# Exchanging the stationary and the streamed operand of P·V, with two V buffers in place of three, in a cached-attention kernel

## Chip, cores, metric

One core of one Trainium2 chip. The metric is the device time of one execution in microseconds (us), as the median over several executions. The profile's span is about 1.8 us shorter than the time of the same run.

## The reference, cut to what matters

```python
# x (8, 4, 448); k_cache, v_cache (8, 8, 8192, 256); wq (448, 4096); wo (4096, 448); all bf16
q = (x @ wq).reshape(8, 4, 16, 256).transpose(0, 2, 1, 3)
k = jnp.repeat(k_cache, 2, axis=1)          # 16 query heads share 8 kv heads
v = jnp.repeat(v_cache, 2, axis=1)
p = softmax(einsum("bhqd,bhkd->bhqk", q, k) * 256 ** -0.5)
o = einsum("bhqk,bhkd->bhqd", p, v)
return o.transpose(0, 2, 1, 3).reshape(8, 4, 4096) @ wo
```

There are 64 items, one per (batch, kv head). Each reads 4 MB of K and 4 MB of V and has only 8 query rows (2 heads x 4 positions).

## The kernel before

All loads are issued by SyncE on one queue, in chunks of 1 MB, K and V alternating. K goes through a ring of six chunk buffers, V through three buffers of a whole item.

```python
for n in range(NIT + 1):                    # NIT = 64 items, NCH = 4 chunks each
    ...                                     # alternating: kdma(n, c), vdma(n - 1, c)
def kdma(n, c):
    e.wait_ge(s_kfree[ks], ku)              # six ring slots
    ...
def vdma(m, pc):
    vs = m % NVBUF                          # NVBUF = 3
    if pc == 0 and m >= NVBUF:
        e.wait_ge(s_pv, m - NVBUF + 1)      # P.V of item m - NVBUF is done
    ...
```

TensorE transposes K tile by tile through PSUM (`stage`; VectorE and ScalarE copy the result to `KT_sb`), multiplies with Q (`ST`), and one item later does the softmax statistics, P·V and the denominator. P·V keeps a V tile stationary and streams P, which it repeats 8 times:

```python
def pe_pv(e, m):
    ...                                     # waits: exp of m, norm of m - 1, V of m
    for half in range(2):
        for t in range(NT):                 # NT = 64 tiles of 128 keys
            pe_mm(e, OT_ps[:, half * OTW:(half + 1) * OTW],
                  lhsT=V_sb[vs][:, t, half * P:(half + 1) * P],
                  rhs=PT_sb[m % 2][:, None, t * QN:(t + 1) * QN].to_broadcast([P, PVREP, QN]),
                  start=(t == 0), stop=(t == NT - 1), ...)     # PVREP = 8, QN = 8

def pe_den(e, m):                           # column sums of P, on all partitions
    pe_mm(e, ST_ps[m % 2][:, 0:NT * QN], lhsT=ones[:, :], rhs=PT_sb[m % 2][:, :], ...)

def dve_part2(e, m):                        # sum over tiles, reciprocal, scale into attnT
    ...

# the end of the TensorE program, after the last K tile
pe_maxT(NIT - 1); pe_bc(NIT - 1)            # P.V of item NIT - 2 came just before
pe_pv(e, NIT - 1); pe_den(e, NIT - 1)
...                                         # 32 matmuls with wo
```

## Time and profile before

Median 1341.24 us of 3 runs (1340.98 to 1341.73).

| what | before |
|---|---|
| bytes in the data queue | 544.3 MB |
| that queue's share of 16 DMA engines | 97.4% |
| TensorE busy, mean clock | 82%, 0.90 |
| packets and bytes of TensorE's instruction queue | 196, 3.21 MB |
| last V chunk landed | 1323.31 us |
| from there to the end of the span | 16.9 us |

The page of the kernel before. The rows of part 2 have one entry for each of 40 equal slices of the span: `DMA` is the busy share of the 16 engines in tenths, `GB/s` what they moved, `PEclk` TensorE's clock in tenths. Part 3 lists the queues: packets, MB, share of 16 engines. In all views PE is TensorE, PEld its weight loads, DVE VectorE, ACT ScalarE, POOL GpSimd and SPq the load queue of SyncE; L139 is line 139 of the kernel file.

```profile
PE 1093.5 (82%) x24932; PEld 1050.4 (78%) x24932; DVE 542.3 (40%) x1161; ACT 556.8 (42%) x577; POOL 0.8 (0%) x7
...
PEclk9969899888998998899898898898898999798998
DMA  7999999999999999999999999999999999999992
GB/s 263 424 411 425 424 424 423 424 425 424 423 425 424 424 424 425 423 423 424 425 423 424 414 419 424 413 422 421 410 424 422 419 419 417 421 410 423 422 399 96
...
q1 hardware_dynamic: 78464, 544.30, 97.4%
q8 instruction: 196, 3.21, 0.9%
```

Between the first slice and the last two, the DMA engines are busy for 90% of the time or more in every slice: this is a DMA-bound kernel. What the average hides is the end. Here is the windows view of the last stretch of loading (start:end, length, then busy time of each engine, clock, DMA share, GB/s):

```profile
1304.00:1321.00 17.00, 10.96 (x293) 10.20 (x290) 5.98 (x15) 5.63 (x6) 0.00 (x0) 0.94 0.51 213
```

For 17 us only half of the DMA capacity is in use. The landing events of the trace say which half: every chunk raises its semaphore sixteen times, and 50 us before the landing of the last chunk eight of these come within about 1 us and the other eight 17 to 19 us later. At 72 us into the run the sixteen lie within 1.7 us; the gap between the eighth and the ninth then grows to 15.4 us at about 1000 us and little after that (16.6 us at 1290 us). So eight of sixteen engines fall behind, and the kernel ends when they end. I call them the late half.

The chain of waits of the kernel before, from the last V load on (start us, length us, what):

```profile
1295.89 27.42 DMA V_sb<-in_v_cache_dram
...
1323.45 6.48 PE bankO L139 x128
1329.93 0.23 PE ST L139
...
1330.18 0.70 DVE dsum L244
...
1330.91 0.21 DVE rden L247
...
1331.14 0.25 DVE attnT L253 x2
...
1331.44 6.24 PE stage L139 x32
...
1337.70 0.61 DVE out_sb L470
```

After the last V chunk come P·V (6.48 us), the denominator matmul with its reduction and reciprocal (1.14 us), the scaling, and the output projection. An ordinary P·V (at 1274 us) took 3.88 us in the chain of waits; this one ran at a low clock.

Three of the costliest groups (line, engine, operation, output<-inputs, shape, count | busy us, mean ns | idle us before them and what ended it):

```profile
L139 PE MATMUL stage<-ident,kq_sb 128*128 128x128 bf16 x5440 | 462.6, 233 | 121.1 <-DMA kq_sb<-in_k_cache_dram 109.3
...
L139 PE MATMUL stage<-ident,K_sb 128*128 128x128 bf16 x2752 | 246.4, 242 | 70.2 <-DMA K_sb<-in_k_cache_dram 65.3
L139 PE MATMUL bankO<-PT_sb,V_sb 128*128 128x64 bf16 x8192 | 266.5, 197 | 14.2 <-issue 10.5
```

TensorE waited 109.3 + 65.3 = 175 us for K, 2.7 us per item of about 20.4 us. It is the second-busiest engine and not the bound. The waits of the load queue itself (who waits <- for whom: us in all, times, longest us):

```profile
SPq L299 <- PE ST L139: 468.0, 213, 5.2
```

This is the K load waiting for a free ring slot. V loads (line 308) do not appear in this view: three V buffers are plenty.

### The profile page before, as it was taken

How to read it: one execution, taken by the hardware profiler on the slowest of the kernel's cores; microseconds unless marked ns; L12 is line 12 of the kernel's file. 1: busy time of each engine (PE TensorE's matmuls, PEld its weight loads, DVE VectorE, ACT ScalarE, POOL GpSimd, SP SyncE). 2: the span in 40 equal slices, each digit the busy share in tenths (PEclk: the TensorE clock that was granted, in tenths of full speed). 3: DMA queues.
4: the chain of work that ended last, by engine and by line, in shares of the span. 5: the costliest groups of instructions: out<-in, count | busy, mean ns of one | idle time of the engine just before them, and what ended most of it. 6: DMA issues, size and time to landing. Idle time of an engine off the chain costs nothing.

```text
span 1340.2 us, 53869 instructions
## 1 busy us (share of the span) xinstructions
PE 1093.5 (82%) x24932; PEld 1050.4 (78%) x24932; DVE 542.3 (40%) x1161; ACT 556.8 (42%) x577; POOL 0.8 (0%) x7
## 2 busy tenths in 40 slices
PE   5878788788788878888878888888888788887886
PEld 4868778788778878877878788878888778787785
DVE  1424344343443443444344443443443444343442
ACT  1524444443443443443444444443443444443441
POOL 0000000000000000000000000000000000000000
PEclk9969899888998998899898898898898999798998
DMA  7999999999999999999999999999999999999992
GB/s 263 424 411 425 424 424 423 424 425 424 423 425 424 424 424 425 423 423 424 425 423 424 414 419 424 413 422 421 410 424 422 419 419 417 421 410 423 422 399 96
DMA packets 78688, 547.74 MB, mean 409 GB/s; under 512 B 8320, under 2 KB 12480, under 8 KB 12480
## 3 DMA queue, kind: packets, MB, share of 16 engines
q1 hardware_dynamic: 78464, 544.30, 97.4%
q8 instruction: 196, 3.21, 0.9%
q14 instruction: 28, 0.23, 0.0%
HBM read 544.24 MB, written 0.03 MB: 406 GB/s over the span
## 4 chain that ended last, share of the span: by engine, by line
DMA 63%; PE 28%; SPq 5%; DVE 2%; issue 2%
DMA kq_sb<-in_k_cache_dram 34%; DMA K_sb<-in_k_cache_dram 25%; PE stage L139 14%; PE bankO L139 8%; PE ST L139 4%; DMA V_sb<-in_v_cache_dram 2%; SPq L284 2%; SPq L308 2%; SPq L299 1%; DVE rmax L422 1%; DMA kq_sb<-in_wq_dram 1%; PE ST L344 1%; PE misc L139 1%; DVE KT_sb L231 1%; DVE dsum L244 0%
## 5 line engine op out<-in xcount | busy, mean ns | idle before, releaser
L229 ACT ACTIVATE KT_sb<-stage 128x1024 bf16<-128x1024 bf16 x512 | 523.7, 1023 | 756.8 <-PE stage L139 756.0
L139 PE MATMUL stage<-ident,kq_sb 128*128 128x128 bf16 x5440 | 462.6, 233 | 121.1 <-DMA kq_sb<-in_k_cache_dram 109.3
L231 DVE COPY KT_sb<-stage 128x1024 bf16<-128x1024 bf16 x512 | 351.1, 690 | 441.3 <-PE stage L139 440.6
L139 PEld LDWEIGHTS stage<-ident,kq_sb 128*128 128x128 bf16 x5440 | 347.1, 104 | 137.1 <-DMA kq_sb<-in_k_cache_dram 116.3
L139 PE MATMUL ST<-QT_sb,KT_sb 128*128 128x8 bf16 x8192 | 368.2, 168 | 16.5 <-issue 16.1
L139 PEld LDWEIGHTS ST<-QT_sb,KT_sb 128*128 128x128 bf16 x8192 | 336.7, 100 | 19.7 <-issue 19.5
L139 PE MATMUL stage<-ident,K_sb 128*128 128x128 bf16 x2752 | 246.4, 242 | 70.2 <-DMA K_sb<-in_k_cache_dram 65.3
L139 PE MATMUL bankO<-PT_sb,V_sb 128*128 128x64 bf16 x8192 | 266.5, 197 | 14.2 <-issue 10.5
L139 PEld LDWEIGHTS bankO<-PT_sb,V_sb 128*128 128x128 bf16 x8192 | 259.0, 101 | 15.7 <-issue 13.3
L139 PEld LDWEIGHTS stage<-ident,K_sb 128*128 128x128 bf16 x2752 | 185.6, 108 | 79.8 <-DMA K_sb<-in_k_cache_dram 69.6
L244 DVE TENSOR_REDUCE dsum<-ST 128x8 f32<-128x512 f32 x64 | 44.3, 692 | 308.8 <-PE ST L139 308.8
L444 DVE TENSOR_TENSOR D_sb<-ST,bc_sb 128x512 f32<-128x512 f32 x64 | 44.3, 692 | 2.2
L422 DVE TENSOR_REDUCE rmax<-ST 128x8 f32<-128x512 f32 x64 | 43.6, 681 | 1.0 <-PE ST L139 1.0
L478 ACT ACTIVATE PT_sb<-D_sb 128x512 bf16<-128x512 f32 x64 | 39.8, 622 | 8.5 <-DVE D_sb L444 8.5
L139 PE MATMUL ST<-PT_sb,ones 128*128 128x512 bf16 x64 | 24.4, 381 | 0.7 <-issue 0.7
L344 PE MATMUL ST<-xT_sb,kq_sb 128*128 128x32 bf16 (+1 forms) x128 | 10.7, 197 | 11.1 <-DMA kq_sb<-in_wq_dram 11.1
L344 PEld LDWEIGHTS ST<-xT_sb,kq_sb 128*128 128x128 bf16 (+1 forms) x128 | 8.3, 107 | 13.5 <-issue 11.2
L139 PE MATMUL misc<-ident,rmax_bf 128*8 128x128 bf16 x64 | 14.1, 221 | 5.8 <-DVE rmax_bf L427 1.5
L431 DVE TENSOR_REDUCE gmax<-misc 8x1 f32<-8x128 bf16 x64 | 17.2, 269 | 2.4 <-PE misc L139 2.4
L253 DVE TENSOR_TENSOR attnT<-bankO,rden 128x8 bf16<-128x8 f32 x128 | 15.4, 161 | 2.3
L434 DVE TENSOR_SCALAR diag<-ident,gmax 8x8 bf16<-8x8 bf16 x64 | 13.9, 217 | 2.3
L247 DVE RECIPROCAL rden<-dsum 128x8 f32<-128x8 f32 x64 | 13.0, 203 | 2.2
(21 smaller groups left out, 64.3 us busy)
## 6 DMA issues: line engine op xcount, KB each, us to landing
V_sb<-in_v_cache_dram SPq DMA_DIRECT2D x256, 1024.0 KB, 22.8
kq_sb<-in_k_cache_dram SPq DMA_DIRECT2D x170, 1024.0 KB, 25.9
K_sb<-in_k_cache_dram SPq DMA_DIRECT2D x86, 1024.0 KB, 25.9
wo_sb<-in_wo_dram SPq DMA_DIRECT2D x2, 1792.0 KB, 31.0
kq_sb<-in_wq_dram SPq DMA_DIRECT2D x3, 1024.0 KB, 6.8
kq_sb<-in_wq_dram SPq DMA_DIRECT2D x1, 512.0 KB, 11.4
x_sb<-in_x_dram SPq DMA_DIRECT2D x1, 28.0 KB, 1.7
out_dram<-out_sb SPq DMA_DIRECT2D x1, 28.0 KB, 1.5
```

The lines of the kernel that those rows point to most:

```text
L139: ins = e.matmul(*args, **kwargs)
L229: ins = e.activation(out=dst, in_=src, func=ACTF.Copy)
L231: ins = e.tensor_copy(out=dst, in_=src)
L244: chain(e, e.tensor_reduce(out=dsum[:, :], in_=ST_ps[m % 2][:, 0:NT * QN].rearrange("p (j q) -> p q j", q=QN), axis=AX.X, op=ALU.add))
L253: ins = e.tensor_tensor(out=attnT[:, c0:c0 + 2, b * Sq:(b + 1) * Sq], in0=OT_ps.rearrange("p (half rq) -> p half rq", half=2)[:, :, r * Sq ...
L284: e.dma_start(wo_sb[:, half_c:, :], wo_v[:, half_c:, :]).then_inc(s_wo, 16)
L308: e.dma_start(V_sb[vs][:, pc * TV:(pc + 1) * TV, :], src).then_inc(s_v[vs], 16)
L344: ins = e.matmul(bank[:, col:col + NR], lhsT=wq_sb[0:w, kc, hc * P:(hc + 1) * P], rhs=xT_sb[0:w, kc, :], start=(kc == 0), stop=(kc == NDC ...
L422: chain(e, e.tensor_reduce(out=rmax[:, :], in_=st[:, 0:NT * QN].rearrange("p (j q) -> p q j", q=QN), axis=AX.X, op=ALU.max))
L431: chain(e, e.tensor_reduce(out=gmax[0:QN, :], in_=MAXT_ps, axis=AX.X, op=ALU.max))
L444: e.tensor_tensor(out=D_sb[m % 2][:, :].rearrange("p (j q) -> p j q", q=QN), in0=st[:, 0:NT * QN].rearrange("p (j q) -> p j q", q=QN), in1 ...
L478: e.activation(out=PT_sb[m % 2][:, :], in_=D_sb[m % 2][:, :], func=ACTF.Exp, scale=scale).then_inc(s_exp, 1)
```

## The change

P becomes stationary (8 columns) and V is streamed (256 columns), so that P·V is 64 matmuls instead of 128. The output then has 8 rows of 256; it is normalized there, and two small transposes bring it to the layout that the output projection wants. The denominator gets its own small VectorE path. One V buffer is given up; the scratch space does not need it, since d_nv3 below ran with three. The last two items keep the old form, but with the denominators moved ahead and fifteen dummy matmuls (`fill`) between the softmax steps.

```diff
-    NVBUF = 3
-    PVREP = 8
+    NVBUF = 2
...
         def pe_pv(e, m):
...
-            for half in range(2):
-                for t in range(NT):
-                    pe_mm(e, OT_ps[:, half * OTW:(half + 1) * OTW],
-                          lhsT=V_sb[vs][:, t, half * P:(half + 1) * P],
-                          rhs=PT_sb[...].to_broadcast([P, PVREP, QN]), ...)
+            for t in range(NT):
+                pe_mm(e, O_ps,                                   # 8 x 256
+                      lhsT=PT_sb[m % 2][:, t * QN:(t + 1) * QN],
+                      rhs=V_sb[vs][:, t, :], ...)
...
+        def pe_ot(e, m):                                         # 2 transposes of 8x128
+        def dve_den(e, m):     # mask with ident, reduce, reciprocal: 8x512
+        def dve_on(e, m):      # O_n = O_ps * rden8, 8x256
+        def dve_otcopy(e, m):  # into attnT
...
-            pe_maxT(NIT - 1)
-            pe_bc(NIT - 1)
-            pe_pv(e, NIT - 1)
-            pe_den(e, NIT - 1)
+            pe_den_vs(e, NIT - 2)
+            fill(9)
+            pe_maxT(NIT - 1)
+            fill(6)
+            pe_bc(NIT - 1)
+            pe_pv_vs(e, NIT - 2)
+            pe_den_vs(e, NIT - 1)
+            pe_pv_vs(e, NIT - 1)
```

More of the change, by code (lines that the diff above doesn't have):

```diff
@@ L90, in bass_standalone__gqa_block_cached__sampling_kernel @@
         rden = sb("rden", [P, QN], FP32)
+        den8 = sb("den8", [P, 1], FP32)
+        rden8 = sb("rden8", [P, 1], FP32)
+        scr = sb("scr", [P, NT * QN], FP32)
+        O_n = [sb(f"O_n{i}", [P, Dh], BF16) for i in range(2)]
         out_sb = sb("out_sb", [P, D], BF16)
@@ L97, in bass_standalone__gqa_block_cached__sampling_kernel @@
         misc_f = misc[:, :].bitcast(FP32)
-        OTW = PVREP * QN
-        OT_ps = bankO[:, 0:2 * OTW]
+        O_ps = bankO[0:QN, 0:Dh]
+        OT2_ps = misc[:, 192:192 + 2 * QN]
         FIN_ps = stage[0][:, :].bitcast(FP32)[0:NR, 0:D]
@@ L127, in bass_standalone__gqa_block_cached__sampling_kernel @@
         s_norm = sem("s_norm")
+        s_on = sem("s_on")
+        s_ot = sem("s_ot")
         s_dve = sem("s_dve")
@@ L199, in pe_den @@
             e.wait_ge(s_exp, m + 1)
-            pe_mm(e, ST_ps[m % 2][:, 0:NT * QN], lhsT=ones[:, :], rhs=PT_sb[m % 2][:, :],
+            pe_mm(e, ST_ps[m % 2][0:QN, 0:NT * QN], lhsT=ones[:, 0:QN], rhs=PT_sb[m % 2][:, :],
                   start=True, stop=True, inc=s_den)
@@ L206, in pe_pv, with pe_den_vs, pe_pv_vs @@
             if m >= 1:
+                e.wait_ge(s_on, m)
+            e.wait_ge(s_v[vs], 16 * NCH * (m // NVBUF + 1))
+            for t in range(NT):
+                pe_mm(e, O_ps,
+                      lhsT=PT_sb[m % 2][:, t * QN:(t + 1) * QN],
+                      rhs=V_sb[vs][:, t, :],
+                      start=(t == 0), stop=(t == NT - 1),
+                      inc=(s_pv if t == NT - 1 else None))
+        OTW = 8 * QN
+        OT_ps = bankO[:, 0:2 * OTW]
+        def pe_den_vs(e, m):
+            e.wait_ge(s_exp, m + 1)
+            pe_mm(e, ST_ps[m % 2][:, 0:NT * QN], lhsT=ones[:, :], rhs=PT_sb[m % 2][:, :],
+                  start=True, stop=True, inc=s_den)
+        def pe_pv_vs(e, m):
+            vs = m % NVBUF
+            e.wait_ge(s_exp, m + 1)
+            if m == NIT - 2:
+                e.wait_ge(s_on, m)
+            else:
                 e.wait_ge(s_norm, m)
@@ L211, in pe_pv @@
                     last_one = (half == 1 and t == NT - 1)
-                    pe_mm(e,
-                          OT_ps[:, half * OTW:(half + 1) * OTW],
+                    pe_mm(e, OT_ps[:, half * OTW:(half + 1) * OTW],
                           lhsT=V_sb[vs][:, t, half * P:(half + 1) * P],
-                          rhs=PT_sb[m % 2][:, None, t * QN:(t + 1) * QN].to_broadcast([P, PVREP, QN]),
-                          start=(t == 0), stop=(t == NT - 1),
-                          inc=(s_pv if last_one else None))
+                          rhs=PT_sb[m % 2][:, None, t * QN:(t + 1) * QN].to_broadcast([P, 8, QN]),
+                          start=(t == 0), stop=(t == NT - 1), inc=(s_pv if last_one else None))
+        def pe_ot(e, m):
+            e.wait_ge(s_on, m + 1)
+            if m >= 1:
+                e.wait_ge(s_norm, m)
+            for h in range(2):
+                pe_mm(e, OT2_ps[:, h * QN:(h + 1) * QN],
+                      lhsT=O_n[m % 2][0:QN, h * P:(h + 1) * P], rhs=ident[0:QN, 0:QN],
+                      is_transpose=True, start=True, stop=True,
+                      inc=(s_ot if h == 1 else None))
         def evac(e, n, g, use_act):
@@ L239, in chain, with dve_part2_vs @@
             e.wait_ge(s_dve, dv_count[0])
-        def dve_part2(e, m):
+        def dve_den(e, m):
+            e.wait_ge(s_den, m + 1)
+            chain(e, e.tensor_tensor(
+                out=scr[0:QN, :].rearrange("p (j q) -> p j q", q=QN),
+                in0=ST_ps[m % 2][0:QN, 0:NT * QN].rearrange("p (j q) -> p j q", q=QN),
+                in1=ident[0:QN, None, 0:QN].to_broadcast([QN, NT, QN]),
+                op=ALU.mult))
+            chain(e, e.tensor_reduce(
+                out=den8[0:QN, 0:1], in_=scr[0:QN, :].rearrange("p (j q) -> p j q", q=QN),
+                axis=AX.XY, op=ALU.add))
+            chain(e, e.reciprocal(rden8[0:QN, :], den8[0:QN, :]))
+        def dve_on(e, m):
+            e.wait_ge(s_pv, m + 1)
+            if m >= 2:
+                e.wait_ge(s_ot, m - 1)
+            e.tensor_scalar(out=O_n[m % 2][0:QN, :], in0=O_ps, scalar1=rden8[0:QN, 0:1],
+                            scalar2=None, op0=ALU.mult).then_inc(s_on, 1)
+        def dve_part2_vs(e, m):
             b, hkv = m // Hkv, m % Hkv
@@ L250, in dve_part2 @@
             for r in range(rep):
-                h = hkv * rep + r
-                c0 = h * 2
+                c0 = (hkv * rep + r) * 2
                 ins = e.tensor_tensor(
@@ L255, in dve_part2 @@
                     in0=OT_ps.rearrange("p (half rq) -> p half rq", half=2)[:, :, r * Sq:(r + 1) * Sq],
-                    in1=rden[:, None, r * Sq:(r + 1) * Sq].to_broadcast([P, 2, Sq]),
-                    op=ALU.mult,
-                )
+                    in1=rden[:, None, r * Sq:(r + 1) * Sq].to_broadcast([P, 2, Sq]), op=ALU.mult)
             ins.then_inc(s_norm, 1)
+        def dve_otcopy(e, m):
+            b, hkv = m // Hkv, m % Hkv
+            e.wait_ge(s_ot, m + 1)
+            src = OT2_ps.rearrange("p (half r s) -> p half r s", half=2, r=rep)
+            dst = attnT[:, hkv * rep * 2:(hkv + 1) * rep * 2, b * Sq:(b + 1) * Sq].rearrange(
+                "p (r half) s -> p half r s", half=2)
+            e.tensor_copy(out=dst, in_=src).then_inc(s_norm, 1)
         block = es.enter_context(nc.Block())
@@ L359, in pe_bc, with pe_denpv @@
                       start=True, stop=True, inc=s_bc)
-            G_MAXT, G_BC, G_PV = min(4, NG - 1), min(6, NG - 1), NG - 1
-            def pe_pvden(m):
+            G_OT, G_MAXT, G_BC, G_PV = min(2, NG - 1), min(4, NG - 1), min(6, NG - 1), NG - 1
+            def pe_denpv(m):
+                pe_den(e, m)
                 pe_pv(e, m)
-                pe_den(e, m)
             NGT = NIT * NG
@@ L370, in _ @@
                 n, g = divmod(G, NG)
-                if g == 0 and n >= 1:
-                    pend += [(G + G_MAXT, lambda m=n - 1: pe_maxT(m)),
-                             (G + G_BC, lambda m=n - 1: pe_bc(m)),
-                             (G + G_PV, lambda m=n - 1: pe_pvden(m))]
+                if g == 0:
+                    if n >= 2:
+                        pend += [(G + G_OT, lambda m=n - 2: pe_ot(e, m))]
+                    if n >= 1:
+                        pend += [(G + G_MAXT, lambda m=n - 1: pe_maxT(m)),
+                                 (G + G_BC, lambda m=n - 1: pe_bc(m))]
+                        if n < NIT - 1:
+                            pend += [(G + G_PV, lambda m=n - 1: pe_denpv(m))]
+                    pend.sort(key=lambda x: x[0])
                 pe_tr_group(e, n, g)
@@ L378, in _ @@
                     if gq == 0 and nq >= 2:
-                        e.wait_ge(s_norm, nq - 1)
+                        e.wait_ge(s_on, nq - 1)
                     pe_qk(e, nq, gq)
@@ L387, in _, with fill @@
                 pend.pop(0)[1]()
+            def fill(k):
+                for _i in range(k):
+                    e.matmul(stage[1][:, :].bitcast(FP32)[:, 0:Dh], lhsT=ident[:, :],
+                             rhs=wo_sb[:, 0, 0:Dh], start=True, stop=True)
+            pe_den_vs(e, NIT - 2)
+            fill(9)
             pe_maxT(NIT - 1)
+            fill(6)
             pe_bc(NIT - 1)
-            pe_pv(e, NIT - 1)
-            pe_den(e, NIT - 1)
+            pe_pv_vs(e, NIT - 2)
+            pe_den_vs(e, NIT - 1)
+            pe_pv_vs(e, NIT - 1)
             e.wait_ge(s_norm, NIT)
@@ L453, in _ @@
                 pend = []
+                if n >= 2:
+                    pend += [(0, lambda m=n - 2: dve_on(e, m)),
+                             (4, lambda m=n - 2: dve_otcopy(e, m))]
                 if n >= 1:
-                    pend = [(1, lambda m=n - 1: dve_sm1(m)),
-                            (2, lambda m=n - 1: dve_sm2(m)),
-                            (3, lambda m=n - 1: dve_sm3(m)),
-                            (7, lambda m=n - 1: dve_part2(e, m))]
+                    pend += [(1, lambda m=n - 1: dve_sm1(m)),
+                             (2, lambda m=n - 1: dve_sm2(m)),
+                             (3, lambda m=n - 1: dve_sm3(m)),
+                             ]
+                    if n < NIT - 1:
+                        pend += [(7, lambda m=n - 1: dve_den(e, m))]
+                pend.sort(key=lambda x: x[0])
                 for i, g in enumerate(dve_groups):
@@ L467, in _ @@
             dve_sm3(NIT - 1)
-            dve_part2(e, NIT - 1)
+            dve_part2_vs(e, NIT - 2)
+            dve_part2_vs(e, NIT - 1)
             e.wait_ge(s_fin, 1)
@@ L476, in act_exp @@
                 if m >= 2:
-                    e.wait_ge(s_den, m - 1)
+                    e.wait_ge(s_pv, m - 1)
                 e.activation(out=PT_sb[m % 2][:, :], in_=D_sb[m % 2][:, :], func=ACTF.Exp,
```

## The prediction

> **What bounds it now: the DMA engines, and of those the late half.** The page's queue table gives 544.3 MB in 97.4% of the 16 engines' span; the forty slices hold 410 to 425 GB/s almost throughout. In the tail the windows view shows DMA share falling to 0.5 and about 205 GB/s from 1304 to 1321 us: half of the engines finish some 17 us before the others. Landing events agree: eight of a chunk's sixteen come early, by up to 17 us. The late half's extra load is, I think, the instruction queue: 196 packets, 3.21 MB, on average 0.93 us each in the trace, so 183 us of engine time, or 23 us on each of eight engines. The Trainium skill, "Runtime: NRT & Kernel Launch", section Instruction fetch mechanics, says that instructions are fetched in 16 KiB blocks of 256; 3.21 MB / 196 = 16 KiB agrees.
>
> TensorE is second: 82% busy, mean clock 0.90. It waits for DMA about 190 us (groups table), some 3 us of the 20.4 us per (batch, kv head).
>
> **What the change does.** P·V becomes 64 matmuls with P as the stationary operand (8 columns) and 256 streamed columns, not 128 with V stationary and 64 streamed columns.
> - PE instructions: per item 128 matmul/weight-load pairs become 64, plus 2 small transposes; about 7,700 of 50,000 instructions go. Estimate: instruction packets 196 to about 166, 28 us of engine time, 3.5 us on each late engine. On the critical path.
> - PE time: P·V takes 3.9 us at full clock now (30 ns each, chain of waits). 64 x 256 streamed columns at the same column rate is an estimated 6.9 us: 3 us MORE per item. That eats most of the PE's slack; it should stay just hidden.
> - DVE: about +0.9 us per item (542 to about 600 us busy); hidden.
> - Two V buffers instead of three: a V load waits for the P·V two items back rather than three. About nine chunks (23 us) stay queued while that P·V runs (7 to 9 us), so the queue should not run dry.
> - Tail: the last two items keep the old form, but both denominators now precede the last P·V. After the last V lands, the denominator matmul, reduction and reciprocal (0.23 + 0.70 + 0.21 us) disappear. The last P·V takes 6.5 us now at clock 0.5; dummy matmuls may warm it partly: say 0.8 us.
>
> **Sum.** 3.5 + 1.2 + 0.8 = 5.5 us: **1336 us, range 1329 to 1350**. Chances: faster by over 2% 0.03, within 2% 0.84, slower by over 2% 0.13.
>
> **What would show it.** Instruction packets near 166; middle slices still at about 420 GB/s; last V landing 3 to 4 us earlier; after it P·V straight to the output projection. P·V matmuls about 107 ns apart; PE busy share up to about 90%, its DMA waits down to 1 us per item or less.
>
> **What would make it wrong.** PE becoming the bound: the skill's "TensorE: Matmul & The Clock Gate", section What's actually happening, gives a half-rate clock after idle; the trace shows 0.5 for 3.4 us stretches in most items. If 8-column matmuls don't count as activity, P·V takes 13.6 us and the kernel is PE-bound, far over 1370 us; middle GB/s would fall. Or the V wait starves the queue: then V issues wait on P·V and the DMA share dips once per item.

## The result, and the profile after

Median 1333.42 us of 10 runs (1332.22 to 1334.85), against 1341.49 us of 12 runs of the kernel before on the same chip. The ratio is 0.994, with a 95% interval of 0.993 to 0.995. A ratio here is the mean time of one kernel's runs over that of the other's of the same rounds, so it is not quite the ratio of the medians quoted. The change is a gain of 8.1 us, clear of noise and well inside 2%.

The page of the changed kernel, the same lines:

```profile
PE 1224.9 (92%) x21103; PEld 1089.0 (82%) x21103; DVE 604.0 (45%) x1223; ACT 552.7 (42%) x577; POOL 0.8 (0%) x7
...
PEclk9889999999999999999999999999999999999899
DMA  6999999999999999999999999999999999999994
GB/s 251 426 410 425 424 425 424 425 424 425 424 425 424 424 423 424 424 422 417 423 421 422 414 425 416 423 421 424 413 417 424 423 419 419 420 424 421 404 423 177
...
q1 hardware_dynamic: 78464, 544.30, 97.9%
q8 instruction: 166, 2.72, 0.7%
```

The data queue is as it was, byte for byte. TensorE is now 92% busy, at a mean clock of 0.977. The instruction queue has lost exactly the 30 packets of the estimate. The windows view of the half-used stretch at the end and the chain of waits from the last V load on:

```profile
1307.00:1317.00 10.00, 9.49 (x206) 8.64 (x204) 4.38 (x10) 2.68 (x3) 0.00 (x0) 0.83 0.51 212
```

```profile
1296.79 21.68 DMA V_sb<-in_v_cache_dram
...
1318.60 3.91 PE bankO L144 x128
...
1322.60 0.25 DVE attnT L307 x2
...
1322.90 6.24 PE stage L144 x32
...
1329.16 0.61 DVE out_sb L552
```

The last V chunk lands at 1318.47 us, 4.8 us earlier. The stretch at half share is shorter. From the landing to the end of the span it takes 13.2 us instead of 16.9 us. The two differences, 4.8 and 3.7 us, add up to the 8.5 us between the two spans.

The groups that answer to those shown of before:

```profile
L144 PE MATMUL stage<-ident,kq_sb 128*128 128x128 bf16 x5440 | 424.0, 221 | 49.4 <-DMA kq_sb<-in_k_cache_dram 48.8
L144 PE MATMUL bankO<-V_sb,PT_sb 128*8 128x256 bf16 x3968 | 446.1, 274 | 3.0 <-DMA V_sb<-in_v_cache_dram 3.0
...
L144 PE MATMUL stage<-ident,K_sb 128*128 128x128 bf16 x2752 | 221.4, 226 | 35.0 <-DMA K_sb<-in_k_cache_dram 33.5
```

P·V costs TensorE 446 us where it cost 267, and the engine's waits for K fall from 175 to 82 us: it pays for the new form out of its slack. The load queue's waits:

```profile
SPq L368 <- PE bankO L144: 549.4, 60, 11.8
SPq L359 <- PE ST L144: 323.0, 185, 2.6
```

V loads (line 368) now do wait for P·V, 549 us in all, the longest 11.8 us. Yet the DMA row above shows no dip. That is a wait that costs nothing, which the runs below check.

### The profile page after: what moved, and what is told of

Same layout as the page of the kernel before. It is cut to its first block, busy times and chain, and to the rows that moved or that the text cites. A ratio compares the mean times of both kernels' runs of the same rounds, so it can differ in the third digit from the quotient of the medians.

```text
span 1331.7 us, 46332 instructions
## 1 busy us (share of the span) xinstructions
PE 1224.9 (92%) x21103; PEld 1089.0 (82%) x21103; DVE 604.0 (45%) x1223; ACT 552.7 (42%) x577; POOL 0.8 (0%) x7
## 4 chain that ended last, share of the span: by engine, by line
DMA 52%; PE 44%; SPq 3%; issue 0%; DVE 0%; DVEq 0%
DMA kq_sb<-in_k_cache_dram 30%; PE bankO L144 18%; PE stage L144 18%; DMA K_sb<-in_k_cache_dram 17%; PE ST L144 7%; DMA V_sb<-in_v_cache_dram 4%; SPq L344 2%; PE misc L144 1%; DMA kq_sb<-in_wq_dram 1%; PE ST L404 1%; SPq L359 1%; SPq L368 0%; SPq L343 0%; SPq L338 0%; DVE out_sb L552 0%
## 5 line engine op out<-in xcount | busy, mean ns | idle before, releaser
L144 PE MATMUL stage<-ident,kq_sb 128*128 128x128 bf16 x5440 | 424.0, 221 | 49.4 <-DMA kq_sb<-in_k_cache_dram 48.8
L144 PE MATMUL bankO<-V_sb,PT_sb 128*8 128x256 bf16 x3968 | 446.1, 274 | 3.0 <-DMA V_sb<-in_v_cache_dram 3.0
L144 PEld LDWEIGHTS bankO<-V_sb,PT_sb 128*8 128x8 bf16 x3968 | 346.2, 87 | 99.3 <-issue 5.9
L144 PEld LDWEIGHTS stage<-ident,kq_sb 128*128 128x128 bf16 x5440 | 314.3, 98 | 67.1 <-DMA kq_sb<-in_k_cache_dram 52.7
L144 PE MATMUL stage<-ident,K_sb 128*128 128x128 bf16 x2752 | 221.4, 226 | 35.0 <-DMA K_sb<-in_k_cache_dram 33.5
L144 PEld LDWEIGHTS stage<-ident,K_sb 128*128 128x128 bf16 x2752 | 165.2, 101 | 44.4 <-DMA K_sb<-in_k_cache_dram 36.0
L279 DVE TENSOR_TENSOR scr<-ST,ident 8x512 f32<-8x512 f32 x62 | 42.1, 679 | 32.6 <-PE ST L144 32.6
L284 DVE TENSOR_REDUCE den<-scr 8x1 f32<-8x512 f32 x62 | 41.8, 674 | 2.1
L293 DVE TENSOR_SCALAR O_n<-bankO,rden 8x256 bf16<-8x256 f32 x62 | 28.7, 463 | 0.0
L144 PE MATMUL ST<-PT_sb,ones 128*8 128x512 bf16 (+1 forms) x64 | 25.7, 401 | 0.0
L404 PE MATMUL ST<-xT_sb,kq_sb 128*128 128x32 bf16 (+1 forms) x128 | 10.7, 197 | 12.0 <-DMA kq_sb<-in_wq_dram 12.0
```

Source lines behind the costliest of these rows:

```text
L144: ins = e.matmul(*args, **kwargs)
L279: chain(e, e.tensor_tensor(out=scr[0:QN, :].rearrange("p (j q) -> p j q", q=QN), in0=ST_ps[m % 2][0:QN, 0:NT * QN].rearrange("p (j q) -> p ...
L284: chain(e, e.tensor_reduce(out=den8[0:QN, 0:1], in_=scr[0:QN, :].rearrange("p (j q) -> p j q", q=QN), axis=AX.XY, op=ALU.add))
L293: e.tensor_scalar(out=O_n[m % 2][0:QN, :], in0=O_ps, scalar1=rden8[0:QN, 0:1], scalar2=None, op0=ALU.mult).then_inc(s_on, 1)
L404: ins = e.matmul(bank[:, col:col + NR], lhsT=wq_sb[0:w, kc, hc * P:(hc + 1) * P], rhs=xT_sb[0:w, kc, :], start=(kc == 0), stop=(kc == NDC ...
```

## The experiments

The open question is where the 4.8 us before the last landing come from. Three theories were set against each other. The *fetch theory*: the late half of the DMA engines carries TensorE's instruction packets, and fewer packets let it finish earlier. The *clock theory*: TensorE is warmer (0.977 against 0.90), and the middle runs more smoothly. The *buffer theory*: the wait of the V loads with two buffers orders the loads better. Times of kernels in one group were taken on one chip with shared runs of the kernel before, which gave 1341.66 to 1341.74 us in every group.

### a_split: the changed kernel with its matmul count restored

```diff
-            for t in range(NT):
-                pe_mm(e, O_ps, lhsT=..., rhs=V_sb[vs][:, t, :], ...)
+            for half in range(2):
+                for t in range(NT):
+                    pe_mm(e, O_ps[:, half * P:(half + 1) * P], lhsT=...,
+                          rhs=V_sb[vs][:, t, half * P:(half + 1) * P], ...)
```

> The changed kernel, but each P.V matmul of 256 streamed columns is cut into two of 128, so that the TensorE program again has as many matmuls as the kernel before; streamed columns, operand roles, buffers and tail stay. Fetch theory (the late half of the DMA engines is slowed by instruction packets): 197 instruction packets instead of 166, the last V chunk lands 3.6 us later than in the changed kernel (31 packets x 0.93 us / 8), about 1322 us, total about 1337. Clock theory (a warmer TensorE brings the gain in the middle): packets do not matter, the mean clock stays at 0.97 to 0.98, the last V lands at 1318.5 and the total stays at 1333.4. Buffer theory (two V buffers order the loads better): also 1333.4.

Measured: 1339.85 us (1339.35 to 1340.14, 5 runs), ratio to before 0.9986 [0.9973, 1.0]. The last V landed at 1324.38 us, at a mean clock of 0.967. Its instruction queue:

```profile
q8 instruction: 197, 3.23, 0.9%
```

With the same operand roles, buffers, tail and nearly the same clock, the gain at the landing is gone altogether. The fetch theory is right about the sign and low about the size: 31 packets cost 5.9 us, not 3.6. The run also adds matmuls and weight loads, so it does not yet settle that it is packets and not TensorE work.

### b_tail: the kernel before with the new tail only

```diff
-            pe_maxT(NIT - 1); pe_bc(NIT - 1)
-            pe_pv(e, NIT - 1); pe_den(e, NIT - 1)
+            pe_den(e, NIT - 2); fill(9); pe_maxT(NIT - 1); fill(6); pe_bc(NIT - 1)
+            pe_pv(e, NIT - 2); pe_den(e, NIT - 1); pe_pv(e, NIT - 1)
```

(and, on VectorE, the scaling of item NIT - 2 moved behind the last softmax.)

> The kernel before with only the changed kernel's tail: the denominators of the last two items before their P.V, the P.V of the last item but one after the last softmax, fifteen dummy matmuls. Fetch theory with its tail share: instruction packets stay at 196, the last V lands at 1323 as before, and from there to the end it takes 13.2 us in place of 16.9, so about 1337.6 us. If the whole gain came from the tail: 1333.4. If the tail alone gains nothing without the new P.V: 1341.

Measured: 1339.40 us (1338.64 to 1341.68, 5 runs), ratio 0.9987 [0.9974, 1.0]; 196 packets; last V at 1323.61 us, and 13.2 us from there to the end in the profiled run, which was the fastest of the five. The tail alone is worth 2.3 us by the medians, with an interval that just reaches 1.0, and up to 3.7 us from the landing on in a run whose last P·V is at full clock. It moves nothing before the landing.

### c_rep16: the kernel before with a busier TensorE

```diff
-    PVREP = 8
+    PVREP = 16
```

> The kernel before with the P operand repeated 16 times instead of 8 (128 streamed columns per P.V matmul): the same number of instructions, but P.V takes about 6.8 us at full clock, as in the changed kernel, and TensorE is busier. Fetch theory: 196 packets, last V lands at 1323, total within 1 us of 1341.5 (up to 2.5 us less if the last P.V runs at a higher clock, more by up to 3 us if it is simply twice as long). Clock theory: the mean clock rises from 0.90 to 0.97 or so and the middle of the kernel gains 3 to 5 us, last V at about 1319.

Measured: 1346.07 us (1345.85 to 1348.15, 5 runs), ratio 1.0036 [1.0024, 1.0049]; 196 packets; last V at 1323.57 us. Its clock, by slices:

```profile
PEclk9989999999999999999999999999999999999999
```

The mean clock is 0.977, the same as in the changed kernel, and the landing did not move by more than 0.3 us. The clock theory fails. The 4 us that this kernel loses lie after the landing, where its last P·V is twice as wide (20.5 us to the end instead of 16.9); that is a little more than the 3 us that the expectation allowed for it.

### d_nv3: the changed kernel with three V buffers

```diff
-    NVBUF = 2
+    NVBUF = 3
```

> The changed kernel with three V buffers instead of two. Fetch theory: 166 packets, late half unchanged, total 1333.4 within 1 us; the wait of V loads for P.V (549 us in total) disappears from the queue and the waits for K slots come back, without effect on the time; the early half's lead grows from some 11 to some 15 us or more. Buffer theory: without the two-buffer wait the last V lands 1 to 3 us later or earlier, total 1335 or 1331.

Measured: 1333.35 us (1333.17 to 1334.73, 5 runs), ratio 0.994 [0.9928, 0.9953]; 166 packets; last V at 1318.15 us. The load queue's waits of this run:

```profile
SPq L359 <- PE ST L144: 554.1, 195, 7.8
```

The 549 us of V waits vanish and K waits take their place, and the time stays. The early half's lead near the end grows from about 11 us back to about 16 us, also at no price. The buffer theory fails, and so does the worry that two buffers would starve the queue.

### e_nop: more TensorE instructions without arithmetic

```diff
             for t in range(NT):
+                e.wait_ge(s_const, 3); e.wait_ge(s_x, 16); e.wait_ge(s_wq, 16 * NDC)
+                e.wait_ge(s_pro_dve, 2); e.wait_ge(s_pro_pe, 2)
                 pe_mm(e, O_ps, ...)
```

> The changed kernel with five waits, each long satisfied, before every P.V matmul of the middle: they add about 8,000 semaphore instructions to the TensorE program and no arithmetic. Fetch theory: 197 packets instead of 166; at the 0.17 us of lateness per packet that the split run showed, the last V lands 5 to 6 us later than in the changed kernel and the total is 1338.5 to 1339.5 (at the 0.117 us of the prediction: 1337). If the split run was slow because of its extra matmuls and weight loads and not because of packets: 1333.4. If the sequencer cannot hide two extra instructions in a 107 ns matmul, P.V gets longer than 7 us and the run says less.

Measured: 1711.15 us (1709.86 to 1713.16, 5 runs), ratio 1.2755. This miss says nothing about what packets cost, for the reason that the expectation named last. The 32 packets more than in the changed kernel hold about 8,200 instructions at 256 each, or two for each of the 62 x 64 matmuls: of the five waits, only two needed an instruction of their own. (The 0.17 us per packet of this expectation and of h_nopv's is a little low: the landings of the split run give 5.9 / 31 = 0.19.) One P·V in the timeline (start, length, group):

```profile
606.24 15.05 PE L144 MATMUL bankO<-V_sb,PT_sb 128*8 128x256 bf16 x64
```

15.05 us instead of 7.0: the two waits added (15.05 - 7.0) / 64 = 126 ns to each matmul, 63 ns apiece if both cost the same. TensorE became the bound, with 97% of the chain. That shows what the changed kernel would look like without its remaining slack.

### f_nofill: the changed kernel without dummy matmuls

```diff
-            fill(9)
...
-            fill(6)
```

> The changed kernel without its fifteen dummy matmuls. If they keep the clock up for the last P.V: the last two P.V run partly at clock 0.5, the time from the last V to the end grows from 13.2 us by 1 to 2.6 us, total 1334.5 to 1336. If the later P.V of the item before is what keeps it warm: total 1333.4 or up to 1 us less. Packets and landing unchanged (166, 1318.5).

Measured: 1333.67 us (1333.10 to 1334.29, 5 runs), ratio 0.9939 [0.9926, 0.9951]; last V at 1317.66 us and 14.3 us to the end. The dummy matmuls are worth nothing that these runs can see. What keeps the clock up for the last P·V is, by elimination, that the P·V of the item before now ends 0.9 us ahead of it (1317.68 and 1318.60 us in the changed kernel) and no longer 5.6 us ahead (1317.83 and 1323.45 us before). No run changes that pause alone, so it is not shown by an experiment; but the 14 kept traces all agree with it. In the nine where the pause before the last P·V was 1.2 us or less, it took 3.9 us; in the three where it was 2.1 to 2.4 us (the repeat below, k_pair, j_balance2), 5.4 us; before, with 5.6 us, 6.5 us. (c_rep16, with a P·V twice as wide, paused for 5.0 us and took 8.95 us, at a mean clock of 0.83.) The kept traces of e_nop, f_nofill and g_balance are of a second profiled execution; the figures here are from it, while the views shown for e_nop and g_balance and the count of 7,419 below are from the first.

### g_balance and j_balance2: moving load between the halves

```diff
# g_balance: V chunk 0 of every second item
+                    for lo, hi in ((0, 112), (112, 120), (120, 128)):
+                        e.dma_start(dst[lo:hi], src[lo:hi]).then_inc(s_v[vs], 16)
# j_balance2: the same chunk by strided rows
+                    rows = [slice(r, 128, 8) for r in range(7)] + [slice(7, 64, 8), slice(71, 128, 8)]
+                    for r in rows:
+                        e.dma_start(dst[r], src[r]).then_inc(s_v[vs], 16)
```

> The changed kernel with one V chunk of every second item issued as 112 partitions plus two pieces of 8 partitions, so that (by the Trainium skill, DMA: Bandwidth and Descriptors) each small piece falls on eight of the sixteen DMA engines only; same bytes. Theory of a late half: if those eight are the early ones, 32 rows of 8 KB x 0.309 us move away from each late engine, the gap between the eighth and ninth landing shrinks from 11 us to 2 us or less, the last V lands up to 9.9 us earlier (about 1309), total 1324 to 1328. If those eight are the late ones: the last V lands 9.9 us later, total about 1343. If there is no fixed late half, nothing changes beyond 1 us.

> The second attempt at moving load between the halves: one V chunk of every second item is issued as nine pieces, seven of 16 rows and two of 8[...]. Same bytes. If the two-fold packet times of the first attempt came from pieces that write other engines' rows, they go away here (fewer than 1,000 packets over 400 ns, as in the kernels before and after, against 7,419 in the first attempt). Then: last V at about 1309 and total 1324 to 1328 if the low eight engines are the early half; 1343 if they are the late half. If the slow packets stay, this way of balancing is closed.

Measured: g_balance 1509.92 us (1507.12 to 1514.5, 4 runs), ratio 1.1256; j_balance2 1527.47 us (1525.03 to 1531.89, 5 runs), ratio 1.1397. Both results were correct. No branch of either expectation gave such a time; only the last sentence of j_balance2's came true, since the slow packets stayed. (The cuts leave out that the wait counts of P·V were raised to match.) Five microseconds just after a split chunk of g_balance was issued (at 608.1 us), in the windows view:

```profile
610.00:615.00 5.00, 3.97 (x88) 3.71 (x84) 3.94 (x9) 3.54 (x5) 0.00 (x0) 1.00 1.05 280
```

The engines are busy and move 280 GB/s instead of 424. An ordinary 8 KB packet takes 309 ns in every kernel here; in these two, 7,419 and 8,255 packets took over 400 ns (7,838 in g_balance's kept trace; half of them under about 560 ns), against 515 before. In g_balance the slow packets come in bursts after the split chunks. I thought that pieces writing other engines' rows were the reason. j_balance2 was meant to avoid most of that and is no better; but its pieces rest on an assumption about which engine writes which rows, which no run here shows, so that reason is not ruled out. The cause of the slow packets stays open, and with it whether the halves can be balanced from the kernel.

### h_nopv: the changed kernel with 7,800 TensorE instructions less

Its output is wrong, which doesn't matter for the time.

```diff
-            for t in range(NT):
-                pe_mm(e, O_ps, lhsT=PT_sb[m % 2][:, t * QN:(t + 1) * QN], rhs=V_sb[vs][:, t, :], ...)
+            pe_mm(e, O_ps, lhsT=PT_sb[m % 2][:, 0:QN], rhs=V_sb[vs][:, 0, :],
+                  start=True, stop=True, inc=s_pv)
```

> Wrong result on purpose: the changed kernel with one P.V matmul per item in place of 64 in the middle (the last two items keep theirs). 7,800 TensorE instructions less, V still loaded and waited for. Fetch theory: about 136 packets, and the last V lands 5 us earlier than in the changed kernel (30 packets x 0.17 us, as the split run showed; 3.5 us at the 0.117 us of the prediction), about 1313.4, total about 1328.5. If TensorE time limited the changed kernel anywhere in the middle, more than that. Theory that packets play no part: the landing stays at 1318.5, since the DMA was the bound already.

Measured: 1328.72 us (1326.97 to 1329.25, 4 runs), ratio 0.9902 [0.9889, 0.9915]; last V at 1311.82 us.

```profile
q8 instruction: 136, 2.23, 0.6%
```

Here TensorE has far less to do and its clock is the lowest of all (0.782), and still the landing moves by 6.6 us, about as much as the same number of packets moved it in a_split the other way. It is more than the 5 us expected, which the expectation would have put down to TensorE time; at the 0.20 us per packet of the line below, 30 packets give 6.0 us, so nothing need be left for that. A DMA-bound kernel got faster by having fewer instructions.

### i_pool: 8,000 instructions on an idle engine

```diff
             e.memset(ones[:, :], 1.0).then_inc(s_const, 1)
+            e.wait_ge(s_pro_pe, 2)
+            for _ in range(8000):
+                e.wait_ge(s_const, 3)
+                e.wait_ge(s_x, 16)
```

> The changed kernel with 8,000 more instructions on GpSimd, which is otherwise idle: satisfied semaphore waits, no arithmetic and no memory access. If instruction blocks of any engine go to the same late half of the DMA engines: about 0.5 MB more in the instruction queues, the last V lands 3.5 to 5 us later, total 1337 to 1339. If those of GpSimd go to other engines: the landing stays at 1318.5 within 1 us and the total at 1333.4, and it is TensorE's instruction queue in particular that counts.

Measured: 1346.22 us (1344.24 to 1350.52, 6 runs), ratio 1.004 [1.0027, 1.0052]; last V at 1329.13 us, 10.7 us later than in the changed kernel.

```profile
q8 instruction: 166, 2.72, 0.7%
q14 instruction: 91, 0.75, 0.1%
```

TensorE's program and its 166 packets are untouched; 63 packets of 8 KB came in the other instruction queue (about 64 bytes for each pair of waits in the loop, so a pair seems to have come out as one instruction), and the kernel lost more than its whole gain. Here no engine on the critical path has a single instruction more, so the fetch traffic itself is what is left (no run separates it from GpSimd's waiting as such). In size both branches of the expectation were wrong: per packet 0.17 us, much like TensorE's of 16 KB, so twice as dear per byte. During these packets (to about 700 us) a single one of the sixteen landings comes last, by 9 to 13 us at 300 to 700 us, and in the whole run the eighth and ninth lie no more than 1.5 us apart, although TensorE's packets go on. So GpSimd's packets seem to fall on fewer and other engines than TensorE's; on which, the trace does not say, and why the two halves do not part again is open.

### k_pair and after_again: a version with fewer instructions, and its yardstick

Two key tiles share a matmul: 16 stationary columns of P, 512 streamed columns of V. Half of the product is cross terms, which nobody reads. The two useful blocks are added by the small output matmuls, which pick rows 0 to 7 and 8 to 15 with slices of the identity.

```diff
-            for t in range(NT):
-                pe_mm(e, O_ps, lhsT=PT_sb[m % 2][:, t * QN:(t + 1) * QN], rhs=V_sb[vs][:, t, :], ...)
+            for t in range(0, NT, 2):
+                pe_mm(e, O_ps, lhsT=PT_sb[m % 2][:, t * QN:(t + 2) * QN],
+                      rhs=V_sb[vs][:, t:t + 2, :], ...)                    # 16 x 512
...
-                pe_mm(e, OT2_ps[:, h * QN:(h + 1) * QN], lhsT=O_n[m % 2][0:QN, h * P:(h + 1) * P],
-                      rhs=ident[0:QN, 0:QN], is_transpose=True, start=True, stop=True, ...)
+                for i in range(2):
+                    pe_mm(e, OT2_ps[:, h * QN:(h + 1) * QN],
+                          lhsT=O_n[m % 2][0:Q2, i * Dh + h * P:i * Dh + (h + 1) * P],
+                          rhs=ident[0:Q2, i * QN:(i + 1) * QN],
+                          start=(i == 0), stop=(i == 1), ...)
...                                         # denominators on 16 partitions, mask of two stacked identities
```

> A version meant to beat both: two key tiles share one P.V matmul (16 stationary columns, 512 streamed columns; the cross terms are computed and thrown away when the two useful blocks are added by the small output matmuls). 32 matmuls per item instead of 64, the same number of streamed columns, four small output matmuls in place of two transposes: 3,700 TensorE instructions less than the changed kernel. Fetch theory: 151 or 152 packets, the last V lands 2.6 us earlier (14.5 packets x 0.18 us), about 1316, total 1330.5 to 1331. TensorE time per item stays at about 7.0 us for P.V; DVE 0.3 us more per item. If packets had no price: 1333.4.

> The changed kernel once more, on the chip of the pair version, as its yardstick: 1333.4 within 0.7 us, 166 packets.

Measured on the same chip: k_pair 1331.15 us (1330.57 to 1332.05, 5 runs), ratio 0.9924 [0.9911, 0.9938], result correct; the changed kernel again 1334.13 us (1332.81 to 1334.53, 5 runs), ratio 0.9942 [0.9929, 0.9954]. The pair version beats both kernels: its slowest run is faster than the changed kernel's fastest beside it, though the intervals of the two ratios overlap.

```profile
q8 instruction: 152, 2.49, 0.7%
```

```profile
643.23 7.07 PE L146 MATMUL bankO<-V_sb,PT_sb 128*16 128x512 bf16 x32
```

Its last V landed at 1314.34 us, against 1317.84 in the repeat; the expected total of 1330.5 to 1331 us was met within 0.2 us. The timeline line shows one P·V: 32 matmuls in 7.07 us, so TensorE gains nothing by it. In both profiled runs the last P·V took 5.45 us or so and the tail 14.7 us; the P·V before it had ended 2.1 and 2.2 us ahead.

### All landings together

| run | instruction packets of TensorE | last V landed, us |
|---|---|---|
| h_nopv | 136 | 1311.82 |
| k_pair | 152 | 1314.34 |
| changed kernel, its repeat, d_nv3, f_nofill | 166 | 1318.47, 1317.84, 1318.15, 1317.66 |
| before, b_tail, c_rep16 | 196 | 1323.31, 1323.61, 1323.57 |
| a_split | 197 | 1324.38 |

A straight line through these ten points has a slope of 0.20 us per packet, and no point lies more than 0.8 us off it. The ten differ in clock (0.78 to 0.98), TensorE busy time (75 to 93%), V buffers, operand roles and tail; the packet count alone orders them.

Two more counts from the same ten traces say how. First, the late half falls behind at a pace that follows the packets: between 350 and 450 us, while that lead still grows, the mean gap between the eighth and ninth landing is 2.5 us with 136 packets in the run, 3.0 with 152, 3.9 to 4.2 with 166 and 5.0 to 5.5 with 196 or 197. Second, data packets are slowed beside instruction packets: of the 8 KB data packets that took over 400 ns, 41 to 48% were under way at the same time as one of TensorE's instruction packets, against 12 to 18% of all 8 KB data packets.

One thing these ten runs cannot separate: the packet count goes with the number of TensorE's instructions. e_nop was to separate them and failed; only i_pool speaks for the packets without TensorE, and it does so on another engine.

## Why the prediction was right

**The bound.** It was the late half of the DMA engines, as stated. The middle slices stayed at 404 to 426 GB/s, and the end moved with the landing of that half.

**Instruction packets.** The count was exact (166). The price was too low: I divided the recorded packet time, 0.93 us, by eight engines and got 0.117 us per packet, 3.5 us in all. The runs show 0.20 us per packet, or 5.5 us between the mean landings at 196 and 166 packets (1323.50 and 1318.03). This term of the sum was mis-sized. Spread over eight engines, 0.20 us on each is about 1.6 us of engine time per packet, more than the 0.93 us that the trace records for it. What I left out is in the traces: the time summed over all packets of the data queue and of TensorE's instruction queue grows by 2.5 us per instruction packet over the ten runs, 0.93 us in the packet itself and the rest in data packets that took longer (317 of 8 KB over 400 ns with 136 packets, 486 to 545 with 196 or 197). How that splits over the engines the traces do not say.

**The tail.** I gave it 2.0 us. The denominator work (1.14 us) left the path as predicted. The clock of the last P·V was worth 2.6 us in the profiled run (6.48 against 3.91 us) and not 0.8; but it varies from run to run, and by medians the whole tail is worth about 2.3 us (b_tail). The dummy matmuls, to which I gave the effect, have no part in it that can be seen (f_nofill): the term's size was near, its reason was not. Both terms were low, and so was the sum: 5.5 us against the 8.1 us measured.

**TensorE time.** The estimate of 6.9 us for the new P·V was right: 6.99 us in the chain of waits of the changed kernel, 109 ns per matmul. The Trainium skill, "TensorE: Matmul & The Clock Gate", section Back-to-back issue gap, gives N / 2.4 + 2.5 ns for isolated matmuls at full clock, an estimate of 109 ns for 256 columns; the trace agrees. The section also says that in a stream of weight loads and matmuls the formula over-counts at large N, with 131 ns for 512 columns; here it does not: k_pair's stream took 7.07 / 32 = 221 ns per matmul of 512 columns. Busy went to 92%, where I said about 90. The waits for K went to 82 us, 1.3 us per item, where I said 1 or less.

**The clock risk.** It did not come. Matmuls with 8 stationary columns keep the clock up (0.977), and so do wider ones with 128 (c_rep16, also 0.977). What they share is a longer dense P·V, and h_nopv, which has almost none, fell to 0.782; whether that is the reason, no run isolates. The same page's section What's actually happening describes a half-rate clock after idle time; the trace agrees where TensorE waits: 128 identical matmuls took 6.48 us at a mean clock of 0.55 and 3.91 us at 1.00.

**V buffers and VectorE.** Both hidden, as said: three buffers give the same time (d_nv3), and VectorE went from 542 to 604 us (I said 600).

## What to carry to other kernels

In a kernel that is bound by DMA, look at how the sixteen landings of one chunk lie apart, not only at the mean DMA share: the kernel ends with its slowest engines, and instruction packets, 0.7 to 0.9% of the DMA engines' time, can decide how late those are. Instructions then have a price even on an engine with slack, or on an idle one; wider matmuls with fewer instructions are worth having although they save no TensorE time. And a new wait with a large total, like the 549 us of V waits here, means nothing until the resource behind it shows a dip.

## What the Trainium skill lacked or had wrong

- "Runtime: NRT & Kernel Launch", section Instruction fetch mechanics: it says instructions come in 16 KiB blocks of 256, and the trace agrees (3.21 MB in 196 packets). It also calls the cost of a block boundary "mostly hidden". As a stall of the sequencer it may be; as traffic it is not: each of TensorE's packets delayed the last landing by 0.20 us, over the range from 136 to 197 packets, and the data packets' time grew with it.
- The same section: nothing says on which DMA engines an engine's instruction blocks are moved. With TensorE's, eight of sixteen landings fall behind by up to 19 us; with 63 packets of 8 KB for GpSimd, one does while they last, and the last landing is 10.7 us later.
- "DMA: Bandwidth & Descriptors", section Why a DMA increments its semaphore by 16 and not by 1, says how many engines a DMA uses, which no run here shows directly, but neither it nor the rest of the page says that a few chunks cut into such pieces can slow many packets. With 64 pieces of 8 rows in 544 MB, 7,419 packets of 8 KB took over 400 ns (309 is ordinary), and the kernel went from 1333 to 1510 us.
- "TensorE: Matmul & The Clock Gate" has no price for a satisfied wait that needs its own instruction. Two of them before each matmul cost 126 ns together (e_nop).
